# K cache rows of 4 KB in two half loads, and scores on four column groups: an attention decode step on one Trainium2 core

## The chip, the core and the metric

The kernel runs on one core of one Trainium2 chip. The metric is the time of one execution on the device, in microseconds; the smaller the better. Times of a kernel are medians of several executions, and the profile is that of one execution.

## What is computed

One decode step of attention with grouped heads: 32 batches of one query each, 32 query heads of 128 over 8 K/V heads, and a window of the last W = 512 keys of a cache of 2048.

```python
q = (x @ wq).reshape(B, 1, 32, 128).transpose(0, 2, 1, 3)      # x: (32, 1, 512)
k = jnp.repeat(k_cache[:, :, 2048 - 512:, :], 4, axis=1)       # cache: (32, 8, 2048, 128)
v = jnp.repeat(v_cache[:, :, 2048 - 512:, :], 4, axis=1)
scores = jnp.einsum("bhqd,bhkd->bhqk", q, k) * 128 ** -0.5
o = jnp.einsum("bhqk,bhkd->bhqd", softmax(scores), v)
out = o.transpose(0, 2, 1, 3).reshape(B, 1, 4096) @ wo         # wo: (4096, 512)
```

All tensors are bfloat16. Per batch the window is 1 MB of K and 1 MB of V; the weights are 4 MB each. Nothing is used twice, so some 75 MB are read once.

## The kernel before, in words

The order of the work is written out by hand, engine by engine, and held together by semaphores; each engine goes through its own program in order.

**SP** issues all loads on one queue (L118 to L163): x, then K of batch 0, the four pieces of wq, V of batch 0, then for each further batch K and V, then the four pieces of wo. K has NK = 4 slots: `load_k(b)` (L129) waits, before it issues, until the transposes of batch b-4 have read their slot (`pe_T3`). V has NV = 12 slots; `load_v(b)` (L137) waits for the P·V of batch b-12. K is laid out with the key on the partition: partition p holds keys 4p to 4p+3 of each of the 8 heads, so a load of K is 128 x 8 rows of 4 keys x 128 x 2 bytes = 1 KB (L132 to L135). V has the same layout and the same 1 KB rows (L142), wo has rows of 512 x 2 bytes = 1 KB (L149), and wq has rows of 1024 x 2 bytes = 2 KB (L124).

**TensorE** makes q (`qt_pass`, L207), and then works batch by batch. `transposes(b)` (L222) turns the K tile of a batch with 32 transposes of 128 x 128 into four PSUM banks of two heads each (`KT_ps`). `s_matmuls(b)` (L242) computes the scores: for each of the 8 heads one matmul whose stationary operand is `QBD`, 128 x 32, with the four queries of that head in four of the 32 columns and zeros elsewhere, and whose moving operand is the head's transposed K, 128 x 512. All eight add up in the same 32 partitions, 32j to 32j+31 for the j-th batch of a quad (j = b mod 4), which is one of the four column groups of the array. Four batches, a quad, so fill the 128 partitions of one `S_ps` bank. Once per quad, behind the transposes of the next quad's second batch, come the four transposes of the probabilities (`pt_transposes`, L262) and then 128 small matmuls with V (`pv_matmuls`, L274). At the end wo is multiplied in, 32 matmuls of 128 x 512 on four column groups in turn (L315), and a last matmul adds the four partial results (L324).

**VectorE** copies three of the four banks of each batch from PSUM to `KT_sb`, 512 columns at a time (L348); **ScalarE** copies the fourth (L405). `KT_sb` has NKT = 3 slots; the copies of batch b wait for the scores of batch b-3. Once per quad, behind the copies of the next quad's first batch, VectorE finds the row maximum (`softmax_a`, L354), ScalarE takes the exponential (L413), and VectorE scales by the reciprocal of the sum (`softmax_b`, L364); ScalarE copies the transposed probabilities (L422) and VectorE the outputs (L370).

**GpSimd** writes the queries of batch b into the diagonal places of `QBD` (L191), which has 8 slots and was set to zero once (L173).

Of the kernel before, what the change touches and what calls it, by code (L numbers as in the profile page):

```python
# [12 lines left out]
def bass_standalone__sliding_block_cached__sampling_kernel(  # L13
# [11 lines left out]
    HQ = HD // DH  # L25
# [17 lines left out]
    with ExitStack() as es:  # L43
# [4 lines left out]
        K_sb = es.enter_context(nc.sbuf_tensor([P, NK, G, KT * DH], BF16))  # L48
        V_sb = es.enter_context(nc.sbuf_tensor([P, NVA, G, KT * DH], BF16))
        KT_sb = es.enter_context(nc.sbuf_tensor([P, NKT, G, W], BF16))  # L50
# [7 lines left out]
        ident = es.enter_context(nc.sbuf_tensor([P, P], BF16))  # L58
        X_sb = es.enter_context(nc.sbuf_tensor([P, D], BF16))
# [15 lines left out]
        sem_k = [es.enter_context(nc.semaphore(f"sem_k{i}")) for i in range(NK)]  # L75
# [15 lines left out]
        pool_R = es.enter_context(nc.semaphore("pool_R"))  # L91
        dve_xT = es.enter_context(nc.semaphore("dve_xT"))
# [21 lines left out]

        def quad_of(b):
            return b // 4

        @block.sync  # L118
        def _(sp):
# [9 lines left out]
            def load_k(b):  # L129
                if b >= NK:  # L130
                    sp.wait_ge(pe_T3, b - NK + 1)
                sp.dma_start(  # L132
                    K_sb[:, b % NK, :, :],
                    k_cache[b, :, SK - W:, :].rearrange("g (p kt) d -> p g (kt d)", kt=KT),
                ).then_inc(sem_k[b % NK], 16)  # L135
# [30 lines left out]
        def _(pool):  # L166
# [5 lines left out]
            ).then_inc(pool_init, 1)  # L172
            pool.memset(QBD[:, :, :, :], 0.0).then_inc(pool_init, 1)  # L173
# [11 lines left out]
            for b in range(B):  # L185
                if b >= NQB:
                    pool.wait_ge(pe_Sb, b - NQB + 1)
                n = b % NQB
                dst = bass.AP(tensor=QBD, offset=n * G * 32, ap=[[qbd_row, P], [36, G], [1, REP]])
                src = bass.AP(tensor=QT_sb, offset=b * HQ, ap=[[qt_row, P], [REP, G], [1, REP]])  # L190
                pool.tensor_copy(dst, src).then_inc(pool_qbd, 1)  # L191

        @block.tensor
        def _(pe):
# [27 lines left out]
            def transposes(b):  # L222
                pe.wait_ge(sem_k[b % NK], 16 * (b // NK + 1))
                for t in range(4):
                    if b >= 1:
                        if t < 3:
                            pe.wait_ge(dve_T, 6 * (b - 1) + 2 * (t + 1))
                        else:
                            pe.wait_ge(act_T, 2 * b)
                    last = None  # L230
                    for half in range(2):
                        g = 2 * t + half
                        for kt in range(KT):
                            last = pe.matmul(  # L234
                                KT_ps[:, t, half * 512 + kt * 128: half * 512 + (kt + 1) * 128],
                                lhsT=K_sb[:, b % NK, g, kt * DH:(kt + 1) * DH],
                                rhs=ident[:, :],
                                start=True, stop=True, is_transpose=True, tile_position=(0, 0),
                            )
                    last.then_inc(pe_T[t], 1)  # L240

            def s_matmuls(b):  # L242
                q = quad_of(b)
                j = b % 4
                pe.wait_ge(pool_qbd, b + 1)
                if j == 0 and q >= 2:
                    pe.wait_ge(act_exp, q - 1)
                last = None
                for g in range(G):
                    if g < 6:  # L250
                        pe.wait_ge(dve_T, 6 * b + g + 1)
                    else:
                        pe.wait_ge(act_T, 2 * b + (g - 6) + 1)
                    last = pe.matmul(  # L254
                        S_ps[32 * j:32 * (j + 1), q % 2, :],
                        lhsT=QBD[:, b % NQB, g, :],
                        rhs=KT_sb[:, b % NKT, g, :],
                        start=(g == 0), stop=(g == G - 1), tile_position=(0, 32 * j),
                    )
                last.then_inc(pe_Sb, 1)  # L260
# [13 lines left out]
            def pv_matmuls(qq):  # L274
# [6 lines left out]
                for j in range(4):  # L281
                    b = 4 * qq + j
                    pe.wait_ge(sem_v[b % NV], 16 * (b // NV + 1))
                    for g in range(G):
                        for kt in range(KT):
# [3 lines left out]
                                rhs=PT_sb[:, qq % 2, kt * 128 + j * 32 + 4 * g: kt * 128 + j * 32 + 4 * g + 4],  # L289
# [8 lines left out]
            s_matmuls(0)  # L298
            for b in range(1, B):
# [4 lines left out]
                s_matmuls(b)  # L304
                if j == 1 and q >= 1:
                    pv_matmuls(q - 1)
            pt_transposes(NQUAD - 1)
# [21 lines left out]
        def _(dve):  # L329
# [11 lines left out]
            def kt_evacs(b):  # L341
                if b >= NKT:
                    dve.wait_ge(pe_Sb, b - NKT + 1)
                for t in range(3):
                    dve.wait_ge(pe_T[t], b + 1)
                    for half in range(2):
                        g = 2 * t + half
                        dve.tensor_copy(  # L348
                            KT_sb[:, b % NKT, g, :], KT_ps[:, t, half * 512:(half + 1) * 512]
                        ).then_inc(dve_T, 1)  # L350
# [7 lines left out]
            def softmax_b(qq):  # L358
# [3 lines left out]
                if qq >= 2:  # L362
                    dve.wait_ge(pe_PT, qq - 1)
                dve.tensor_scalar(  # L364
                    P_bf[:, qq % 2, :], P_f32[:, qq % 2, :], recip[:, qq:qq + 1], None, op0=ALU.mult
# [28 lines left out]
        def _(act):  # L394
# [3 lines left out]
            def kt_evacs(b):  # L398
                if b >= NKT:
                    act.wait_ge(pe_Sb, b - NKT + 1)  # L400
                for t in range(3, 4):
                    act.wait_ge(pe_T[t], b + 1)
                    for half in range(2):
                        g = 2 * t + half
                        act.activation(  # L405
                            KT_sb[:, b % NKT, g, :], KT_ps[:, t, half * 512:(half + 1) * 512], ACTF.Copy
                        ).then_inc(act_T, 1)
# [62 lines left out]
```

## Time and profile before

| what | us |
|---|---|
| median of 3 runs | 229.69 |
| lowest and highest run | 229.09, 232.55 |
| span of the profiled execution | 228.2 |
| last load (wo, fourth piece) lands at | 222.46 |
| TensorE busy | 176.6 |
| VectorE busy | 90.0 |
| ScalarE busy | 48.1 |

No own time is listed for the profiled execution beside its span; against the median of the runs, what lies around the span comes to 229.69 - 228.2 = 1.5 us, and against the lowest run to 0.9 us.

How to read it: the page gives the busy time of each engine, then the span in 40 slices of 5.7 us with the busy share of each engine in tenths, the granted clock of TensorE, the share of the 16 DMA engines and what they moved in GB/s. The chain that ended last is followed back from the last instruction. A group of instructions is one row: line, engine, operation, what it writes and reads, shape and count; then busy time, mean duration of one in ns, and the idle time before it with what ended it.

### The profile page before, as it was taken

The numbers are of one execution on the slowest core, as the hardware profiler recorded it, in microseconds if no ns is written. First come the engines' busy times: TensorE is split into PE (matmuls) and PEld (weight loads), VectorE is DVE, ScalarE is ACT, GpSimd is POOL, SyncE is SP. The second block draws the span as 40 slices with busy tenths as digits, with TensorE's granted clock in tenths as the row PEclk, the third lists the DMA queues.
The fourth block names the chain that finished last, engine by engine and source line by source line (L and its number), as shares of the span: only waits on it lengthen the run. The fifth ranks groups of instructions, "written<-read, shape, count | busy, mean of one in ns | idle before, by whom it ended". The sixth has DMA issues, their size and how long they took to land.

```text
span 228.2 us, 5628 instructions
## 1 busy us (share of the span) xinstructions
PE 176.6 (77%) x2501; PEld 124.7 (55%) x2501; DVE 90.0 (39%) x237; ACT 48.1 (21%) x93; POOL 9.4 (4%) x43
## 2 busy tenths in 40 slices
PE   0184968669869986995997996699669799999482
PEld 0182555447635753575564964477437656695340
DVE  0047333351535243633275243524353317644212
ACT  2000103122113211320133021321132013403203
POOL 5002000000000000000000000000000000000000
PEclk9998879999997999797699889889997859979855
DMA  6999999999999999999999999999999999999950
GB/s 188 386 385 348 348 348 349 348 348 350 349 347 348 349 347 348 348 348 348 348 348 348 347 348 348 348 348 348 347 347 348 347 348 347 349 345 329 350 183 6
DMA packets 72950, 75.90 MB, mean 333 GB/s; under 512 B 1184, under 2 KB 70880, under 8 KB 72928
## 3 DMA queue, kind: packets, MB, share of 16 engines
q1 hardware_dynamic: 72928, 75.57, 103.7%
q8 instruction: 19, 0.31, 0.6%
q14 instruction: 3, 0.02, 0.0%
HBM read 75.53 MB, written 0.03 MB: 331 GB/s over the span
## 4 chain that ended last, share of the span: by engine, by line
DMA 53%; PE 26%; SPq 16%; issue 2%; DVEq 0%; DVE 0%; ACT 0%
DMA K_sb<-in_k_cache_dram 48%; PE KT_ps L234 12%; PE S_ps L254 7%; PE QO_ps L286 6%; SPq L142 6%; DMA wo_sb<-in_wo_dram 5%; SPq L132 5%; SPq L149 4%; SPq L124 2%; PE PT_ps L266 1%; PE KT_ps L315 0%; DVEq L43 0%; DVE X_sb L389 0%; PE QO_ps L324 0%; ACT out_sb L441 0%
## 5 line engine op out<-in xcount | busy, mean ns | idle before, releaser
L234 PE MATMUL KT_ps<-ident,K_sb 128*128 128x128 bf16 x1024 | 74.3, 240 | 29.7 <-DMA K_sb<-in_k_cache_dram 25.6
L348 DVE COPY KT_sb<-KT_ps 128x512 bf16<-128x512 bf16 x192 | 68.0, 418 | 68.0 <-PE KT_ps L234 67.3
L234 PEld LDWEIGHTS KT_ps<-ident,K_sb 128*128 128x128 bf16 x1024 | 67.8, 108 | 42.1 <-DMA K_sb<-in_k_cache_dram 34.9
L254 PE MATMUL S_ps<-KT_sb,QBD 128*32 128x512 bf16 x256 | 68.2, 414 | 2.8 <-POOL QBD L191 2.8
L405 ACT ACTIVATE KT_sb<-KT_ps 128x512 bf16<-128x512 bf16 x64 | 34.7, 594 | 161.6 <-PE KT_ps L234 161.6
L254 PEld LDWEIGHTS S_ps<-KT_sb,QBD 128*32 128x32 bf16 x256 | 23.7, 102 | 34.8 <-issue 8.2
L286 PEld LDWEIGHTS QO_ps<-PT_sb,V_sb 128*128 128x128 bf16 x768 | 20.0, 97 | 3.2 <-ACT PT_sb L422 2.1
L286 PE MATMUL QO_ps<-PT_sb,V_sb 128*128 128x4 bf16 x768 | 20.7, 165 | 0.8 <-ACT PT_sb L422 0.7
L370 DVE CAST oT_sb<-QO_ps 128x128 bf16<-128x128 f32 x8 | 5.8, 719 | 38.8 <-PE QO_ps L286 38.8
L191 POOL COPY QBD<-QT_sb 128x32 bf16<-128x32 bf16 x32 | 6.3, 209 | 152.7 <-PE S_ps L254 135.8
L214 PE MATMUL QO_ps<-xT_sb,big_sb 128*128 128x32 bf16 x128 | 4.1, 185 | 8.4 <-DMA big_sb<-in_wq_dram 8.3
L336 DVE CAST QT_sb<-QO_ps 128x512 bf16<-128x512 f32 x2 | 4.8, 2393 | 13.0 <-PE QO_ps L214 13.0
L214 PEld LDWEIGHTS QO_ps<-xT_sb,big_sb 128*128 128x128 bf16 x128 | 3.8, 103 | 8.7 <-issue 6.7
L286 PEld LDWEIGHTS QO_ps<-PT_sb,big_sb 128*128 128x128 bf16 x256 | 6.5, 96 | 0.8 <-ACT PT_sb L422 0.8
L286 PE MATMUL QO_ps<-PT_sb,big_sb 128*128 128x4 bf16 x256 | 6.7, 164 | 0.0
L413 ACT ACTIVATE P_f_56<-S_ps,negmax 128x512 f32<-128x512 f32 x8 | 5.5, 687 | 4.0 <-DVE negmax L356 4.0
L354 DVE TENSOR_REDUCE maxv<-S_ps 128x1 f32<-128x512 f32 x8 | 5.5, 682 | 1.0 <-PE S_ps L254 1.0
L266 PE MATMUL PT_ps<-ident,P_bf 128*128 128x128 bf16 x32 | 3.6, 242 | 2.5 <-DVE P_bf L364 2.5
L422 ACT ACTIVATE PT_sb<-PT_ps 128x512 bf16<-128x512 bf16 x8 | 4.8, 604 | 1.2 <-PE PT_ps L266 1.2
L315 PE MATMUL KT_ps<-wo_sb,oT_sb 128*32 128x512 bf16 x32 | 3.9, 626 | 0.9 <-DVE oT_sb L370 0.8
L266 PEld LDWEIGHTS PT_ps<-ident,P_bf 128*128 128x128 bf16 x32 | 2.5, 111 | 3.0 <-DVE P_bf L364 3.0
L364 DVE TENSOR_SCALAR P_bf<-P_f_56,recip 128x512 bf16<-128x512 f32 x8 | 3.9, 486 | 0.3
(25 smaller groups left out, 14.7 us busy)
## 6 DMA issues: line engine op xcount, KB each, us to landing
K_sb<-in_k_cache_dram SPq DMA_DIRECT2D x32, 1024.0 KB, 12.1
V_sb<-in_v_cache_dram SPq DMA_DIRECT2D x24, 1024.0 KB, 12.0
big_sb<-in_v_cache_dram SPq DMA_DIRECT2D x8, 1024.0 KB, 12.0
big_sb<-in_wq_dram SPq DMA_DIRECT2D x4, 1024.0 KB, 10.8
wo_sb<-in_wo_dram SPq DMA_DIRECT2D x4, 1024.0 KB, 12.0
x_sb<-in_x_dram SPq DMA_DIRECT2D x1, 32.0 KB, 1.6
out_dram<-out_sb SPq DMA_DIRECT2D x1, 32.0 KB, 1.5
```

The lines of the kernel that those rows point to most:

```text
L132: sp.dma_start(K_sb[:, b % NK, :, :], k_cache[b, :, SK - W:, :].rearrange("g (p kt) d -> p g (kt d)", kt=KT),).then_inc(sem_k[b % NK], 16)
L142: sp.dma_start(v_slot(b)[:, :, :], v_cache[b, :, SK - W:, :].rearrange("g (p kt) d -> p g (kt d)", kt=KT),).then_inc(sem_v[b % NV], 16)
L149: sp.dma_start(wo_sb[:, c * 8:(c + 1) * 8, :], wo[c * 1024:(c + 1) * 1024, :].rearrange("(h d) n -> d h n", d=P),).then_inc(sem_wo[c], 16)
L191: pool.tensor_copy(dst, src).then_inc(pool_qbd, 1)
L214: last = pe.matmul(QO_ps[:, hl * 32:(hl + 1) * 32], lhsT=wq_sb[:, kt, h * DH:(h + 1) * DH], rhs=xT_sb[:, kt, :], start=(kt == 0), stop=(kt ...
L234: last = pe.matmul(KT_ps[:, t, half * 512 + kt * 128: half * 512 + (kt + 1) * 128], lhsT=K_sb[:, b % NK, g, kt * DH:(kt + 1) * DH], rhs=id ...
L254: last = pe.matmul(S_ps[32 * j:32 * (j + 1), q % 2, :], lhsT=QBD[:, b % NQB, g, :], rhs=KT_sb[:, b % NKT, g, :], start=(g == 0), stop=(g = ...
L266: last = pe.matmul(PT_ps[:, kt * 128:(kt + 1) * 128], lhsT=P_bf[:, qq % 2, kt * 128:(kt + 1) * 128], rhs=ident[:, :], start=True, stop=Tru ...
L286: last = pe.matmul(QO_ps[:, j * 32 + 4 * g: j * 32 + 4 * g + 4], lhsT=v_slot(b)[:, g, kt * DH:(kt + 1) * DH], rhs=PT_sb[:, qq % 2, kt * 12 ...
L348: dve.tensor_copy(KT_sb[:, b % NKT, g, :], KT_ps[:, t, half * 512:(half + 1) * 512]).then_inc(dve_T, 1)
L370: dve.tensor_copy(oT_sb[:, :, 4 * qq:4 * qq + 4].rearrange("p h j -> p j h"), QO_ps[:, 0:128].rearrange("p (j h) -> p j h", h=HQ),).then_i ...
L405: act.activation(KT_sb[:, b % NKT, g, :], KT_ps[:, t, half * 512:(half + 1) * 512], ACTF.Copy).then_inc(act_T, 1)
```

## The change

K of one batch comes in two DMAs of four heads each. Within a half, the partition is no longer a block of keys for all heads, but the pair (block of 16 keys, head): partition 4s + g holds keys 16s to 16s+15 of head g, 16 x 128 x 2 bytes = 4 KB that lie together in the cache. Each half has a semaphore of its own, and the first two banks of transposes wait for the first half only, the last two for the second. A transpose of 128 columns now holds one key of each of the 32 blocks of four heads; it is made against a permutation matrix (`perm`, built by GpSimd at the start) which sorts its output into head, then block. A half therefore lies in `KT_sb` as 16 keys x 4 heads x 32 blocks, and the moving operand of a score matmul is 16 pieces of 32 elements, 128 elements apart. The keys of a score row are then in the order (key in block, block); the scaling of the probabilities, which reads P_f32 and writes P_bf, puts them back into the order of V, by reading with a step.

The scores of head g go to the 32 partitions of column group g mod 4, and within it to rows 16(g div 4) + 4j for the batch j of the quad. The sum over PSUM runs over the four batches of a quad and two heads, and the rows of a quad are sorted differently (`prow`).

VectorE and ScalarE copy a whole bank of 1024 columns at once (three copies and one per batch instead of six and two). And `s_matmuls(b - 1)` stands behind `transposes(b)`; before, `s_matmuls(b)` stood behind `transposes(b)`.

The diff, cut to its core:

```diff
         def load_k(b):
             if b >= NK:
                 sp.wait_ge(pe_T3, b - NK + 1)
-            sp.dma_start(
-                K_sb[:, b % NK, :, :],
-                k_cache[b, :, SK - W:, :].rearrange("g (p kt) d -> p g (kt d)", kt=KT),
-            ).then_inc(sem_k[b % NK], 16)
+            for h in range(2):
+                sp.dma_start(
+                    K_sb[:, b % NK, h * 16 * DH:(h + 1) * 16 * DH],
+                    k_cache[b, 4 * h:4 * h + 4, SK - W:, :].rearrange("g (s r) d -> s g (r d)", s=32),
+                ).then_inc(sem_k[b % NK][h], 16)
...
+            pool.memset(perm[:, :, :], 0.0).then_inc(pool_perm, 1)
+            pool.wait_ge(pool_perm, 1)
+            pool.affine_select(
+                out=perm[:, :, :], in_=perm[:, :, :], compare_op=ALU.not_equal, fill=1.0,
+                base=0, pattern=[[-1, 4], [-4, 32]], channel_multiplier=1,
+            ).then_inc(pool_perm, 1)
...
         def transposes(b):
-            pe.wait_ge(sem_k[b % NK], 16 * (b // NK + 1))
             for t in range(4):
+                if t % 2 == 0:
+                    pe.wait_ge(sem_k[b % NK][t // 2], 16 * (b // NK + 1))
...
-                            rhs=ident[:, :],
+                        rhs=perm[:, :, :],
...
         def s_matmuls(b):
...
+            pe.wait_ge(dve_T, 3 * b + 3)
+            pe.wait_ge(act_T, b + 1)
             for g in range(G):
-                if g < 6:
-                    pe.wait_ge(dve_T, 6 * b + g + 1)
-                else:
-                    pe.wait_ge(act_T, 2 * b + (g - 6) + 1)
                 last = pe.matmul(
-                    S_ps[32 * j:32 * (j + 1), q % 2, :],
+                    S_ps[32 * (g % 4):32 * (g % 4) + 32, q % 2, :],
                     lhsT=QBD[:, b % NQB, g, :],
-                    rhs=KT_sb[:, b % NKT, g, :],
-                    start=(g == 0), stop=(g == G - 1), tile_position=(0, 32 * j),
+                    rhs=KT_sb[:, b % NKT, g // 4, :, g % 4, :],
+                    start=(j == 0 and g < 4), stop=(j == 3 and g >= 4), tile_position=(0, 32 * (g % 4)),
                 )
...
-        s_matmuls(0)
         for b in range(1, B):
             q, j = divmod(b, 4)
             transposes(b)
             if j == 1 and q >= 1:
                 pt_transposes(q - 1)
-            s_matmuls(b)
+            s_matmuls(b - 1)
             if j == 1 and q >= 1:
                 pv_matmuls(q - 1)
+        s_matmuls(B - 1)
         pt_transposes(NQUAD - 1)
         pv_matmuls(NQUAD - 1)
...
             for t in range(3):
                 dve.wait_ge(pe_T[t], b + 1)
-                for half in range(2):
-                    g = 2 * t + half
-                    dve.tensor_copy(
-                        KT_sb[:, b % NKT, g, :], KT_ps[:, t, half * 512:(half + 1) * 512]
-                    ).then_inc(dve_T, 1)
+                dve.tensor_copy(
+                    KT_sb[:, b % NKT, t // 2, 8 * (t % 2):8 * (t % 2) + 8, :, :], KT_ps[:, t, :]
+                ).then_inc(dve_T, 1)
...
             dve.tensor_scalar(
-                P_bf[:, qq % 2, :], P_f32[:, qq % 2, :], recip[:, qq:qq + 1], None, op0=ALU.mult
+                P_bf[:, qq % 2, :].rearrange("p (kt s u) -> p kt s u", kt=KT, s=32),
+                P_f32[:, qq % 2, :].rearrange("p (u kt s) -> p kt s u", kt=KT, s=32),
+                recip[:, qq:qq + 1], None, op0=ALU.mult,
             ).then_inc(dve_P, 1)
```

How the change moves instructions, at three places. First the start of SP's queue; a row is a line, the destination and source, and the shape in partitions x rows x elements. Before:

```order
L120 DMA x_sb<-in_x_dram 32x512
L132 DMA K_sb<-in_k_cache_dram 128x8x512
L124 DMA big_sb<-in_wq_dram 128x4x1024 x4
L142 DMA V_sb<-in_v_cache_dram 128x8x512
L132 DMA K_sb<-in_k_cache_dram 128x8x512
```

and now:

```order
L125 DMA x_sb<-in_x_dram 32x512
L138 DMA K_sb<-in_k_cache_dram 128x1x2048 x2
L129 DMA big_sb<-in_wq_dram 128x4x1024 x4
L148 DMA V_sb<-in_v_cache_dram 128x8x512
L138 DMA K_sb<-in_k_cache_dram 128x1x2048 x2
```

The order of the loads is the same; a K load of 8 rows of 512 elements per partition has become two of one row of 2048.

Second the start of TensorE's program: x transposed, the two passes of q (`QO_ps`), the transposes of K (`KT_ps`) and the scores (`S_ps`). Before:

```order
L198 MATMUL S_ps<-ident,x_sb 128x32 x4
L214 MATMUL QO_ps<-xT_sb,big_sb 128x32 x64
L234 MATMUL KT_ps<-ident,K_sb 128x128 x32
L214 MATMUL QO_ps<-xT_sb,big_sb 128x32 x64
L254 MATMUL S_ps<-KT_sb,QBD 32x512 x8
L234 MATMUL KT_ps<-ident,K_sb 128x128 x32
```

and now:

```order
L215 MATMUL S_ps<-ident,x_sb 128x32 x4
L231 MATMUL QO_ps<-xT_sb,big_sb 128x32 x64
L253 MATMUL KT_ps<-perm,K_sb 128x128 x32
L231 MATMUL QO_ps<-xT_sb,big_sb 128x32 x64
L253 MATMUL KT_ps<-perm,K_sb 128x128 x32
L271 MATMUL S_ps<-KT_sb,QBD 32x512 x8
```

The scores of batch 0 have moved behind the transposes of batch 1, and so all through: each batch's scores stand behind the next batch's transposes.

Third the end of TensorE's program, from the transposes of batch 31 on. Before:

```order
L234 MATMUL KT_ps<-ident,K_sb 128x128 x32
L254 MATMUL S_ps<-KT_sb,QBD 32x512 x8
L266 MATMUL PT_ps<-ident,P_bf 128x128 x4
L286 MATMUL QO_ps<-PT_sb,V_sb 128x4 x128
L315 MATMUL KT_ps<-wo_sb,oT_sb 32x512 x32
L324 MATMUL QO_ps<-X_sb,R_sb 32x512
```

and now:

```order
L253 MATMUL KT_ps<-perm,K_sb 128x128 x32
L271 MATMUL S_ps<-KT_sb,QBD 32x512 x16
L283 MATMUL PT_ps<-ident,P_bf 128x128 x4
L303 MATMUL QO_ps<-PT_sb,V_sb 128x4 x128
L332 MATMUL KT_ps<-wo_sb,oT_sb 32x512 x32
L341 MATMUL QO_ps<-X_sb,R_sb 32x512
```

Between the last transposes and the softmax of the last quad there are now the scores of two batches, 30 and 31, instead of one.

50 lines of the change are left out of this document (29 added, 21 removed).

## The prediction

> **What bounds the kernel now.** First I read the page: the busy time of the engines, the two lines on the DMA engines, and the chain that ended last.
>
> ```profile
> span 228.2 us, 5628 instructions
> ...
> PE 176.6 (77%) x2501; PEld 124.7 (55%) x2501; DVE 90.0 (39%) x237; ACT 48.1 (21%) x93; POOL 9.4 (4%) x43
> ...
> DMA  6999999999999999999999999999999999999950
> GB/s 188 386 385 348 348 348 349 348 348 350 349 347 348 349 347 348 348 348 348 348 348 348 347 348 348 348 348 348 347 347 348 347 348 347 349 345 329 350 183 6
> ...
> DMA 53%; PE 26%; SPq 16%; issue 2%; DVEq 0%; DVE 0%; ACT 0%
> ```
>
> From the second slice to the 38th the DMA engines are never under 90% busy, and for some 190 us they move the same 348 GB/s. Nothing else in the page is so even. TensorE stands in the chain with 26%, so the next question is whether it ever holds the loads up. The steady stretch of SP's queue, in order of time (start, duration, instruction):
>
> ```profile
> 161.68 2.92 SPq L142 DMA_DIRECT2D V_sb<-in_v_cache_dram  x1
> 164.64 2.90 SPq L132 DMA_DIRECT2D K_sb<-in_k_cache_dram  x1
> 167.59 2.90 SPq L142 DMA_DIRECT2D V_sb<-in_v_cache_dram  x1
> ```
>
> SP issues load after load without a gap, 2.9 us each, the time that 1.049 MB take at 348 GB/s (3.01 us). At the start, with empty queues, the same instruction took less:
>
> ```profile
> 1.19 0.41 SPq L132 DMA_DIRECT2D K_sb<-in_k_cache_dram  x1
> ```
>
> and the page's list of DMA issues (count, size, us to landing):
>
> ```profile
> K_sb<-in_k_cache_dram SPq DMA_DIRECT2D x32, 1024.0 KB, 12.1
> ```
>
> 0.41 us against 2.9: the issue isn't slow, it waits for room. 12.1 us from issue to landing are four loads in flight. So the stream of loads is full, SP is ahead of it, and the kernel ends when 75.5 MB have passed. **What sets the rate** is seen in the mean over two stretches: 30 to 200 us, where K and V pass in 1 KB rows, and 6 to 16 us, where wq passes in 2 KB rows.
>
> ```profile
> DMA packets 58399, 59.15 MB, mean 348 GB/s; under 512 B 902, under 2 KB 58380, under 8 KB 58380
> ...
> DMA packets 1938, 3.87 MB, mean 387 GB/s; under 512 B 50, under 2 KB 50, under 8 KB 1938
> ```
>
> Both times the engines are full, and the rate differs with the packet. One engine of 16 spends 1024 x 16 / 348 = 47.1 ns on a packet of 1 KB and 2048 x 16 / 387 = 84.7 ns on one of 2 KB: 37.6 ns for each KB and about 9.5 ns for the packet itself.
>
> **The loads of K.** 32 x 1.049 = 33.55 MB are 32768 packets of 1 KB, 2048 on each engine: 2048 x 47.1 = 96.5 us of the stream. Now they are 8192 packets of 4 KB, 512 on each. The trace has no such packet. Bounds: if 2 KB already reaches a ceiling, K passes at 387 GB/s, 86.7 us; if the 9.5 ns vanish too, 4 x 37.6 = 150.4 ns, 77.0 us. I take the straight line through the two rows, 84.7 + 2 x 37.6 = 159.9 ns (410 GB/s): 512 x 159.9 = 81.9 us, a gain of **14.6 us** (9.8 to 19.5). [...]
>
> 32 more DMAs bring 32 more of the small packets per engine that follow a load. Each costs nothing to 47.1 ns; with four bytes it is nearest to the 9.5 ns of a packet without its KBs: **+0.3 us** (0 to 1.5). SP issues twice as many loads of K, at 0.41 us where there is room: 32 more are 13 us of a queue that has some 210; they are hidden while SP is ahead.
>
> **The scores on four column groups.** Before and after are compared in these groups (busy us, mean ns; idle before):
>
> ```profile
> L234 PE MATMUL KT_ps<-ident,K_sb 128*128 128x128 bf16 x1024 | 74.3, 240 | 29.7 <-DMA K_sb<-in_k_cache_dram 25.6 <-issue 4.0
> L254 PE MATMUL S_ps<-KT_sb,QBD 128*32 128x512 bf16 x256 | 68.2, 414 | 2.8 <-POOL QBD L191 2.8
> L348 DVE COPY KT_sb<-KT_ps 128x512 bf16<-128x512 bf16 x192 | 68.0, 418 | 68.0 <-PE KT_ps L234 67.3
> L405 ACT ACTIVATE KT_sb<-KT_ps 128x512 bf16<-128x512 bf16 x64 | 34.7, 594 | 161.6 <-PE KT_ps L234 161.6
> L364 DVE TENSOR_SCALAR P_bf<-P_f_56,recip 128x512 bf16<-128x512 f32 x8 | 3.9, 486 | 0.3
> L336 DVE CAST QT_sb<-QO_ps 128x512 bf16<-128x512 f32 x2 | 4.8, 2393 | 13.0 <-PE QO_ps L214 13.0
> ```
>
> The transposes already idle 25.6 us for K. What four groups bring is seen at the end, where the matmuls with wo go round the four groups, at a granted clock of 0.50 (the number before the last two in the stage's row):
>
> ```profile
> 220.02 0.16 PEld L315 LDWEIGHTS KT_ps<-wo_sb,oT_sb 128*32 128x32 bf16 x4 [0.27 <-issue]
> 220.44 0.16 PEld L315 LDWEIGHTS KT_ps<-wo_sb,oT_sb 128*32 128x32 bf16 x4 [0.27 <-issue]
> ```
>
> ```profile
> 220.00:228.20 8.20, 4.08 (x33) 0.97 (x25) 1.36 (x2) 1.76 (x3) 0.00 (x0) 0.50 0.06 18
> ```
>
> Four matmuls every 0.43 us at half clock, so the eight of a batch take 0.85 us, and half of that at full clock, where L254 takes 68.2 / 32 = 2.1 us now. TensorE loses 41 to 54 us of work. It stands beside the loads: a batch needs 2.6 + 3.0 = 5.6 us of the stream (before 6.0). The parts of a quad, as long as they were at half clock, where the transposes took 3.43 us instead of 1.96:
>
> ```profile
> 170.51 3.43 PE L234 MATMUL KT_ps<-ident,K_sb 128*128 128x128 bf16 x32 [2.18 <-DMA K_sb<-in_k_cache_dram]
> ...
> 173.73 0.59 PE L266 MATMUL PT_ps<-ident,P_bf 128*128 128x128 bf16 x4
> ...
> 176.09 3.36 PE L286 MATMUL QO_ps<-PT_sb,big_sb 128*128 128x4 bf16 x128
> ```
>
> A whole quad at half clock: 4 x (3.43 + 0.85) + 0.59 + 3.36 = 21.1 us, against 4 x 5.6 = 22.4 us of loads. So the scores are worth **0 us**, since the loads cover them. If the cover were gone they would count in full. The moving operand in pieces of 32 elements has no row; below it is no slower, above as slow as the stepped copy L336, 4.67 ns an element. Pieces of 64 bytes are nearer to contiguous; I take no loss.
>
> **Waits and moves.** `s_matmuls(b-1)` now stands behind the wait for K of batch b, and so starts up to 5.6 us later. Who waits: the softmax, but on VectorE it stands behind the copies of that same batch b anyway; the copies, which need the scores of three batches back; and `QBD` with 8 slots. 0 us each. `load_k(b)` waits for the transposes of b-4, with up to three pairs of loads (16.7 us) behind that batch; V has 12 slots. Loads of K now hold fewer packets, so SP will run further ahead and really stand in this wait, at no cost. The copies of 1024 columns cost at most two of 512; VectorE is busy 90 of 228 us. `perm` is built while TensorE waits for wq. 0 us.
>
> **The end.** From the last K on, TensorE's rows, and the chain's row of the last wo:
>
> ```profile
> 207.86 1.96 PE L234 MATMUL KT_ps<-ident,K_sb 128*128 128x128 bf16 x32 [0.53 <-DMA K_sb<-in_k_cache_dram]
> 209.75 1.90 PE L254 MATMUL S_ps<-KT_sb,QBD 128*32 128x512 bf16 x8
> 214.15 0.40 PE L266 MATMUL PT_ps<-ident,P_bf 128*128 128x128 bf16 x4 [2.50 <-DVE P_bf L364]
> ...
> 219.61 3.93 PE L315 MATMUL KT_ps<-wo_sb,oT_sb 128*32 128x512 bf16 x32 [0.80 <-DVE oT_sb L370]
> ```
>
> ```profile
> 210.95 11.51 DMA wo_sb<-in_wo_dram
> ```
>
> wo's last piece lands at 222.46, 14.6 us behind the last K, and so it will stay, since V and wo are unchanged. The computation has a chain beside that: 11.75 us from 207.86 to 219.61, then six rounds of four matmuls at 0.43 us, 14.3 us in all. It has only 0.3 us to spare. Changes in it: half of the transposes wait for the last half load (-0.98 us), the scores of two batches stand between instead of one (2 x 0.43 to 2 x 0.85 plus the wait for a 1.08 us copy, against 1.9: 0 to +0.9), and the stepped read of the probabilities (L364) costs 0.49 us as now up to 2.39 as L336, 0 to +1.9. Together -1.0 to +1.8; I take 0, since L364 keeps its contiguous write, which L336 lacks.
>
> **Sum.** Span 228.2 - 14.6 + 0.3 = 213.9 us. Around the span lie 1.5 us to the median of the runs: **215.4 us**, 6% less.
>
> **Rivals.** *The rate has a ceiling at 387 GB/s.* For it: only that rate is seen, and it may be the memory's and not the packet's. Against: it is a step of the size that a fixed cost per packet gives. Gain 9.8, with the small packets 229.7 - 9.8 + 0.3 = **220.2 us**.
>
> *Packets of 4 KB bring nothing*, because they are cut into 1 KB after all, or K's place in memory limits it to what it has: K stays at 348 GB/s, **230.0 us**. Against: wq's rows arrive as packets of their full 2 KB, and order and DMA shape say one row of 2048 elements. [...]
>
> *The big packets are slower*, since four heads that lie 512 KB apart (2048 x 128 x 2 bytes) are read by turns and get in each other's way. Its place is K's share of the stream; it decides from 188 ns a packet (4 x 47.1), where K gains nothing. The only bigger packets in the trace are the 16 KB of instruction loads:
>
> ```profile
> q8 instruction: 19, 0.31, 0.6%
> ```
>
> 0.6% of 16 x 228.2 us over 19 packets is 1.15 us each, 0.29 us for 4 KB; at that price K takes 147 us, the kernel **281 us**. Against: K and V before have the same step between heads, and run as fast as wo, which has not (351 GB/s):
>
> ```profile
> 210.00:215.00 5.00, 2.04 (x12) 0.78 (x10) 2.16 (x7) 2.19 (x5) 0.00 (x0) 1.00 1.08 351
> ```
>
> [...]
>
> **Chances.** The forecast 0.79; the ceiling 0.11; nothing gained 0.06; slower 0.04. The first two are both faster by over 2% (under 225.1 us; 2% is about what a measurement of this kernel can tell from no change): 0.90 faster, 0.06 the same, 0.04 slower. The range takes in the ceiling and half of the way to the upper gain: **213 to 220.5 us**; the forecast's own is 213 to 217.5.
>
> **What would show it.** Right: some 49 thousand packets instead of 72.9 thousand, those under 2 KB down from 70.9 to some 38.6 thousand; 2.097 MB in 5.6 us, some 376 GB/s, in the middle slices; the last wo landing near 208 us; score matmuls busy under 30 us; waits of SP for the transposes with gaps between its issues, and DMA slices still full. Wrong: slices at 348 or about 366 GB/s (ceiling); slices under 9 in the middle, which would mean that TensorE holds the loads up; and for the end, wo landed long before its last matmuls start.

## The result, and the profile after

The changed kernel takes **217.37 us** (median of 4 runs, 217.21 to 217.76) against 229.47 us before (median of 4, 229.09 to 232.55): a ratio of 0.948, 95% interval 0.9466 to 0.9495. The forecast was 215.4 us, the range 213 to 220.5. Ratios here and below leave out executions more than 1.5% above the fastest of their kernel, so they are not quite the quotient of the medians.

The page of the kernel after: busy time, the 40 slices, the packets, and the chain that ended last.

```profile
span 215.7 us, 5573 instructions
...
PE 149.2 (69%) x2501; PEld 120.0 (56%) x2501; DVE 89.7 (42%) x141; ACT 46.3 (21%) x61; POOL 10.0 (5%) x45
...
DMA  5999999999999999999999999999999999999910
GB/s 166 369 397 374 375 376 375 375 375 375 375 378 376 377 376 378 378 377 376 377 377 375 378 376 378 373 377 377 375 377 377 376 372 376 376 366 319 354 67 6
DMA packets 48886, 75.91 MB, mean 352 GB/s; under 512 B 1696, under 2 KB 38624, under 8 KB 48864
...
DMA 41%; PE 34%; SPq 13%; issue 5%; ACT 4%; DVE 1%; DVEq 0%; ACTq 0%
```

The DMA line is as full as it was, slice by slice, and every slice in the middle now moves 372 to 378 GB/s instead of some 348. The packets are 24 thousand fewer, and those under 2 KB have gone from 70880 to 38624: K's 32768 are gone, 8192 larger ones and 512 small ones have come. The mean over the even stretch (30 to 185 us):

```profile
DMA packets 36720, 58.32 MB, mean 376 GB/s; under 512 B 1328, under 2 KB 29602, under 8 KB 36701
```

A pair of K and V, 2.097 MB, takes 2.097 / 376 = 5.58 us; 3.01 of them are V's, taken at the 348 GB/s of before, so 2.57 us are left for the 16 packets of 4 KB of each engine: 160 ns a packet. The groups that answer to those of before:

```profile
L253 PE MATMUL KT_ps<-perm,K_sb 128*128 128x128 bf16 x1024 | 90.7, 266 | 39.5 <-DMA K_sb<-in_k_cache_dram 32.9
L363 DVE COPY KT_sb<-KT_ps 128x1024 bf16<-128x1024 bf16 x96 | 63.8, 690 | 50.2 <-PE KT_ps L253 49.0
L420 ACT ACTIVATE KT_sb<-KT_ps 128x1024 bf16<-128x1024 bf16 x32 | 32.8, 1024 | 148.7 <-PE KT_ps L253 148.7
L271 PE MATMUL S_ps<-KT_sb,QBD 128*32 128x512 bf16 x256 | 23.3, 446 | 0.7 <-ACT KT_sb L420 0.7
L379 DVE TENSOR_SCALAR P_bf<-P_f,recip 128x512 bf16<-128x512 f32 x8 | 5.9, 742 | 0.3
```

The scores take 23.3 us instead of 68.2, but TensorE as a whole only 27 us less: its transposes went from 74.3 to 90.7 us. They are as many and of the same shape; the granted clock of TensorE is lower (0.785 on average against 0.882), with 149.2 us busy instead of 176.6. TensorE still waits for K, 32.9 us. SP's queue in the steady state:

```profile
162.39 0.59 SPq L148 DMA_DIRECT2D V_sb<-in_v_cache_dram  x1
163.02 5.08 SPq L138 DMA_DIRECT2D K_sb<-in_k_cache_dram  x2
168.15 0.59 SPq L148 DMA_DIRECT2D V_sb<-in_v_cache_dram  x1
```

V's issue takes 0.59 us instead of 2.9, but the two issues of K take 5.1, and again there is no gap between one row and the next: SP's time has moved from V to K. Part of K's time is `load_k`'s wait for the transposes, which the forecast named. The view of SP's waits (us in total, times, longest) has it before, and now:

```profile
SPq L132 <- PE KT_ps L234: 39.8, 19, 3.5
```

```profile
SPq L138 <- PE KT_ps L253: 51.4, 16, 4.4
```

So SP stood in this wait before the change too; the forecast took its 2.9 us for a wait for room alone. The wait is 12 us longer now, and the DMA slices stay full behind it.

At the end: the last wo, and TensorE's rows from the last transposes on (the first two rows are from the view of one line: issues of wo from first to last, and time to landing, of which the last one's is the least).

```profile
L155 SPq DMA_DIRECT2D wo_sb<-in_wo_dram x4: 2802/3702/5020, 185.1 to 197.6; - x4
...
DMA to landing us min/median/max: 11.3/12.8/15.2
```

```profile
193.44 2.61 PE L253 MATMUL KT_ps<-perm,K_sb 128*128 128x128 bf16 x32
195.97 0.62 PE L271 MATMUL S_ps<-KT_sb,QBD 128*32 128x512 bf16 x8
197.31 0.61 PE L271 MATMUL S_ps<-KT_sb,QBD 128*32 128x512 bf16 x8 [0.72 <-ACT KT_sb L420]
200.69 0.40 PE L283 MATMUL PT_ps<-ident,P_bf 128*128 128x128 bf16 x4 [2.77 <-DVE P_bf L379]
...
206.16 0.62 PE L332 MATMUL KT_ps<-wo_sb,oT_sb 128*32 128x512 bf16 x3 [0.80 <-DVE oT_sb L387]
207.43 3.59 PE L332 MATMUL KT_ps<-wo_sb,oT_sb 128*32 128x512 bf16 x29 [0.66 <-issue]
```

The last wo lands at 197.6 + 11.3 = 208.9 us, and the last matmul with wo ends at 207.43 + 3.59 = 211.0, 2.1 us later; before it was 223.6 - 222.5 = 1.1 us. In this execution TensorE no longer waits for wo at the end: wo waits for TensorE.

### The profile page after: what moved, and what is told of

Read it like the earlier page. It is cut to its first block, busy times and chain, and to the rows that moved or that the text cites. A ratio compares the mean times of both kernels' runs of the same rounds, so it can differ in the third digit from the quotient of the medians.

```text
span 215.7 us, 5573 instructions
## 1 busy us (share of the span) xinstructions
PE 149.2 (69%) x2501; PEld 120.0 (56%) x2501; DVE 89.7 (42%) x141; ACT 46.3 (21%) x61; POOL 10.0 (5%) x45
## 2 busy tenths in 40 slices
DMA packets 48886, 75.91 MB, mean 352 GB/s; under 512 B 1696, under 2 KB 38624, under 8 KB 48864
## 4 chain that ended last, share of the span: by engine, by line
DMA 41%; PE 34%; SPq 13%; issue 5%; ACT 4%; DVE 1%; DVEq 0%; ACTq 0%
DMA K_sb<-in_k_cache_dram 41%; PE KT_ps L253 18%; PE QO_ps L303 13%; SPq L138 10%; SPq L148 3%; ACT PT_sb L437 2%; PE KT_ps L332 2%; ACT KT_sb L420 2%; SPq L129 1%; PE S_ps L271 1%; DVE P_bf L379 0%; DVEq L43 0%; DVE oT_sb L387 0%; DVE maxv L369 0%; DVE X_sb L406 0%
## 5 line engine op out<-in xcount | busy, mean ns | idle before, releaser
L253 PE MATMUL KT_ps<-perm,K_sb 128*128 128x128 bf16 x1024 | 90.7, 266 | 39.5 <-DMA K_sb<-in_k_cache_dram 32.9
L253 PEld LDWEIGHTS KT_ps<-perm,K_sb 128*128 128x128 bf16 x1024 | 81.8, 123 | 56.1 <-DMA K_sb<-in_k_cache_dram 48.1
L363 DVE COPY KT_sb<-KT_ps 128x1024 bf16<-128x1024 bf16 x96 | 63.8, 690 | 50.2 <-PE KT_ps L253 49.0
L420 ACT ACTIVATE KT_sb<-KT_ps 128x1024 bf16<-128x1024 bf16 x32 | 32.8, 1024 | 148.7 <-PE KT_ps L253 148.7
L271 PE MATMUL S_ps<-KT_sb,QBD 128*32 128x512 bf16 x256 | 23.3, 446 | 0.7 <-ACT KT_sb L420 0.7
L271 PEld LDWEIGHTS S_ps<-KT_sb,QBD 128*32 128x32 bf16 x256 | 4.0, 98 | 5.4 <-issue 3.3
L428 ACT ACTIVATE P_f<-S_ps,negmax 128x512 f32<-128x512 f32 x8 | 5.5, 687 | 4.5 <-DVE negmax L371 4.5
L379 DVE TENSOR_SCALAR P_bf<-P_f,recip 128x512 bf16<-128x512 f32 x8 | 5.9, 742 | 0.3
```

The source lines that it names most:

```text
L253: last = pe.matmul(KT_ps[:, t, i * 128:(i + 1) * 128], lhsT=K_sb[:, b % NK, r * DH:(r + 1) * DH], rhs=perm[:, :, :], start=True, stop=True ...
L271: last = pe.matmul(S_ps[32 * (g % 4):32 * (g % 4) + 32, q % 2, :], lhsT=QBD[:, b % NQB, g, :], rhs=KT_sb[:, b % NKT, g // 4, :, g % 4, :], ...
L363: dve.tensor_copy(KT_sb[:, b % NKT, t // 2, 8 * (t % 2):8 * (t % 2) + 8, :, :], KT_ps[:, t, :]).then_inc(dve_T, 1)
L420: act.activation(KT_sb[:, b % NKT, t // 2, 8 * (t % 2):8 * (t % 2) + 8, :, :], KT_ps[:, t, :], ACTF.Copy).then_inc(act_T, 1)
```

## The experiments

Two theories could explain the 12 us. **Packets:** the loads set the pace, and an engine spends 9.5 ns on a packet and 37.6 ns on each KB of it. **TensorE:** the time came from the scores on four groups. A third was open for the size: a **ceiling** of the rate near what was seen.

### The groups alone, with the old loads

The change with K's load, its place in memory and the transposes against the identity as before:

```diff
-                for h in range(2):
-                    sp.dma_start(
-                        K_sb[:, b % NK, h * 16 * DH:(h + 1) * 16 * DH],
-                        k_cache[b, 4 * h:4 * h + 4, SK - W:, :].rearrange("g (s r) d -> s g (r d)", s=32),
-                    ).then_inc(sem_k[b % NK][h], 16)
+                sp.dma_start(
+                    K_sb[:, b % NK, :, :],
+                    k_cache[b, :, SK - W:, :].rearrange("g (p kt) d -> p g (kt d)", kt=KT),
+                ).then_inc(sem_k[b % NK][0], 16)
...
-                            rhs=perm[:, :, :],
+                            rhs=ident[:, :],
...
-                        rhs=KT_sb[:, b % NKT, g // 4, :, g % 4, :],
+                        rhs=KT_sb[:, b % NKT, g, :],
```

> The other part of the change alone: scores on four column groups, one batch late, and copies of 1024 columns as in the change, but K in one load of 1 KB rows with the key on the partition, as before. Theory (packets: an engine spends 9.5 ns on a packet and 37.6 ns on each KB): K's packets are back at 47.1 ns for 1 KB, which gives back 14.6 - 0.3 us, so 229 to 232 us, with 348 GB/s in the middle, although TensorE keeps its short scores (about 23 us busy instead of 68). Rival (TensorE: the time came from the scores): stays at 217 to 219 us.

Measured: 229.62 us (10 runs), ratio to before 0.9996, interval 0.9978 to 1.0014. The scores' group, and the mean of 30 to 185 us:

```profile
L268 PE MATMUL S_ps<-KT_sb,QBD 128*32 128x512 bf16 x256 | 24.0, 460 | 0.7 <-ACT KT_sb L415 0.7
```

```profile
DMA packets 53373, 54.04 MB, mean 349 GB/s; under 512 B 823, under 2 KB 53357, under 8 KB 53357
```

TensorE has lost 44 us of scores (its transposes, at 92.2 us, took 18 of them back) and the kernel's time is the same within 0.2%. The TensorE theory falls.

### The loads alone, with one column group

The change with `QBD`, the output rows and the sums of the scores as before, one group of 32 partitions for each batch:

```diff
-                        S_ps[32 * (g % 4):32 * (g % 4) + 32, q % 2, :],
+                        S_ps[32 * j:32 * (j + 1), q % 2, :],
...
-                        start=(j == 0 and g < 4), stop=(j == 3 and g >= 4), tile_position=(0, 32 * (g % 4)),
+                        start=(g == 0), stop=(g == G - 1), tile_position=(0, 32 * j),
...
-            return 32 * (g % 4) + 16 * (g // 4) + 4 * j
+            return 32 * j + 4 * g
```

> The change's loads of K alone: 4 KB rows in two halves, but all eight score matmuls of a batch in one column group, 32j, as before. Theory (packets): the loads still set the pace, 376 GB/s in the middle; a quad of TensorE is 4 x (1.96 + 2.1) + 4 = 20 us at full clock against 22.4 us of loads, hidden; at the end two batches of scores stand in the chain, each 1.3 us longer, of which about 0.5 us hides behind a copy: 218 to 220.5 us. Rival (TensorE): 228 to 231 us, like the kernel before.

Measured: 219.53 us, ratio 0.9562, interval 0.9531 to 0.9593.

```profile
L266 PE MATMUL S_ps<-KT_sb,QBD 128*32 128x512 bf16 x256 | 63.2, 394 | 0.0
```

```profile
DMA packets 36747, 58.36 MB, mean 377 GB/s; under 512 B 1330, under 2 KB 29624, under 8 KB 36728
```

With 63 us of scores the loads run at the same 377 GB/s. So 10.2 of the 12.1 us come without the groups; the groups bring the other 2 us, and only together with the loads. In the two profiles 1.6 us of that show at the end: in this kernel two batches of scores stand behind the last transposes with 1.6 us each, and the first matmul with wo starts at 207.8 us instead of 206.2:

```profile
196.32 3.22 PE L266 MATMUL S_ps<-KT_sb,QBD 128*32 128x512 bf16 x16
...
207.77 0.61 PE L327 MATMUL KT_ps<-wo_sb,oT_sb 128*32 128x512 bf16 x3 [0.81 <-DVE oT_sb L382]
```

### Rows of 2 KB

Each half in two loads of 2 KB rows, four DMAs for a K:

```diff
-                    sp.dma_start(
-                        K_sb[:, b % NK, h * 16 * DH:(h + 1) * 16 * DH],
-                        k_cache[b, 4 * h:4 * h + 4, SK - W:, :].rearrange("g (s r) d -> s g (r d)", s=32),
-                    ).then_inc(sem_k[b % NK][h], 16)
+                    for c in range(2):
+                        sp.dma_start(
+                            K_sb[:, b % NK, (2 * h + c) * 8 * DH:(2 * h + c + 1) * 8 * DH],
+                            k_cache[b, 4 * h:4 * h + 4, SK - W:, :].rearrange(
+                                "g (s c r) d -> c s g (r d)", s=32, c=2
+                            )[c],
+                        ).then_inc(sem_k[b % NK][h], 16)
...
```

> The change with each half load of K cut into two loads of 2 KB rows; K lies in the same places. Theory (9.5 ns a packet, 37.6 ns a KB): 1024 packets of 84.7 ns on each engine instead of 512 of 159.9, 4.8 us more, and 64 more small packets per engine at about 10 ns, 0.6 us more: 222 to 223.5 us, some 364 GB/s in the middle. Rival (a ceiling that 2 KB packets already reach): 217.4 to 218.5 us. Rival (TensorE): 217.4 us.

Measured: 222.99 us, ratio 0.9713, interval 0.9667 to 0.9759.

```profile
DMA packets 43563, 56.77 MB, mean 366 GB/s; under 512 B 2151, under 2 KB 29773, under 8 KB 43545
```

2.097 / 366 - 3.01 = 2.72 us for 32 packets, 85 ns each: the row of wq in the profile before (84.7 ns). No ceiling at 2 KB; the forecast's first rival falls.

### Rows of 8 KB

One load for a K, 16 blocks of 32 keys x 8 heads on the partitions:

```diff
-                for h in range(2):
-                    sp.dma_start(
-                        K_sb[:, b % NK, h * 16 * DH:(h + 1) * 16 * DH],
-                        k_cache[b, 4 * h:4 * h + 4, SK - W:, :].rearrange("g (s r) d -> s g (r d)", s=32),
-                    ).then_inc(sem_k[b % NK][h], 16)
+                sp.dma_start(
+                    K_sb[:, b % NK, :],
+                    k_cache[b, :, SK - W:, :].rearrange("g (s r) d -> s g (r d)", s=16),
+                ).then_inc(sem_k[b % NK][0], 16)
...
```

> The line drawn one step further: K in one load of 8 KB rows, 16 blocks of 32 keys x 8 heads on the partitions, everything else as in the change. Theory (9.5 ns a packet, 37.6 ns a KB): 256 packets of 310 ns on each engine, 79.4 us instead of 81.9, and 32 small packets fewer: 2.8 us less for the loads, less 0 to 1 us at the end, where the transposes wait for a whole load: 214.5 to 216 us, some 382 GB/s in the middle. Rival (a ceiling near 410 GB/s): 217 to 218.5 us.

Measured: **330.62 us** (325.92 to 337.32), ratio 1.4255. Both expectations were wrong. The mean of 60 to 260 us:

```profile
DMA packets 26522, 46.91 MB, mean 235 GB/s; under 512 B 714, under 2 KB 23678, under 8 KB 23678
```

The engines are full, over 90% busy in 39 of the stretch's 40 slices, and slow: in the packet records one of 8 KB lasts 581 ns on average, and even V's packets of 1 KB beside them 71 ns instead of 50. Something in the order of the reads, or in the size of the rows, gets in its own way. Four more kernels look for it, all from this one.

The same places, each row cut into two loads of 4 KB:

```diff
-                sp.dma_start(
-                    K_sb[:, b % NK, :],
-                    k_cache[b, :, SK - W:, :].rearrange("g (s r) d -> s g (r d)", s=16),
-                ).then_inc(sem_k[b % NK][0], 16)
+                for c in range(2):
+                    sp.dma_start(
+                        K_sb[:, b % NK, c * 16 * DH:(c + 1) * 16 * DH],
+                        k_cache[b, :, SK - W:, :].rearrange("g (s c r) d -> c s g (r d)", s=16, c=2)[c],
+                    ).then_inc(sem_k[b % NK][0], 16)
...
```

> The kernel with 8 KB rows, each row cut into two loads of 4 KB rows; every partition keeps its place in the cache, 16 blocks of 32 keys x 8 heads. Theory 1 (it was the packet of 8 KB that was slow, 581 ns on average): packets of 4 KB at 160 ns are back and so is the change's time, 217 to 219 us. Theory 2 (it was the order in which the engines go through the cache, eight heads 512 KB apart by turns): the packets stay slow, 290 ns or so for 4 KB, and the time stays near 330 us, in any case above 260.

Measured: 311.41 us (308.52 to 328.81). Packets of 4 KB are slow here, 279 ns on average in the records of the slowest of the four executions (328.81 us), against 168 in those of the change. So packets of 4 KB alone are no cure.

Eight KB, but four heads by turns:

```diff
-                sp.dma_start(
-                    K_sb[:, b % NK, :],
-                    k_cache[b, :, SK - W:, :].rearrange("g (s r) d -> s g (r d)", s=16),
-                ).then_inc(sem_k[b % NK][0], 16)
+                for h in range(2):
+                    sp.dma_start(
+                        K_sb[64 * h:64 * h + 64, b % NK, :],
+                        k_cache[b, 4 * h:4 * h + 4, SK - W:, :].rearrange("g (s r) d -> s g (r d)", s=16),
+                    ).then_inc(sem_k[b % NK][0], 16)
...
```

> Rows of 8 KB again, but in two loads of four heads each (64 partitions, 16 blocks of 32 keys x 4 heads), so that an engine goes through four heads 512 KB apart by turns and not eight; the rest is as in the kernel with 8 KB rows. Theory 1 (eight heads by turns are what is slow, and four are not): packets of 310 ns, the line of 9.5 ns and 37.6 ns a KB holds up to 8 KB: 214 to 217 us. Theory 2 (steps of 8 KB from engine to engine, or rows of 8 KB, are what is slow, whatever the number of heads): 300 us or more. Between the two, 225 to 290 us: the number of heads counts, but so does the rest.

Measured: 302.95 us (291.14 to 306.15). Four heads by turns alone are no cure either. The turns are those of the rows in the load; which rows an engine takes shows in no view. The change, which is fast, has both, packets of 4 KB and four heads, and its blocks lie 4 KB apart and not 8; which of these it takes together, no run separates.

Pieces 128 KB apart instead of heads 512 KB apart (near), and, from that, rows in one run with no such steps (flat). Neither loads the right keys; the two read the same 1 MB for a batch, in the same rows of 8 KB, and differ in nothing but the order of the rows:

```diff
+                near = k_cache[b, 0:2, :, :].rearrange("a t d -> (a t d)")
                 sp.dma_start(
-                    K_sb[:, b % NK, :],
-                    k_cache[b, :, SK - W:, :].rearrange("g (s r) d -> s g (r d)", s=16),
+                    K_sb[:, b % NK, :], near.rearrange("(g s f) -> s g f", g=8, s=16),
                 ).then_inc(sem_k[b % NK][0], 16)
```

```diff
-                    K_sb[:, b % NK, :], near.rearrange("(g s f) -> s g f", g=8, s=16),
+                    K_sb[:, b % NK, :], near.rearrange("(p f) -> p f", p=P),
```

> The kernel with one load of K in 8 KB rows, but what it loads as the eight heads of a batch are eight neighbouring pieces of 128 KB of the cache instead of eight pieces 512 KB apart. It leaves the right keys out, so only its time is read. Theory 1 (the step of 512 KB between rows that follow each other is what is slow once rows are long): packets of 310 ns, 214 to 217 us. Theory 2 (rows of 8 KB are slow whatever they lie beside): 300 us or more.

> The same once more, with the rows of 8 KB taken straight through 1 MB of the cache, each partition behind the one before. It leaves the right keys out, so only its time is read. Theory 1 (the step of 512 KB is slow): 214 to 217 us, as with the step of 128 KB. Theory 2 (rows of 8 KB are slow): 300 us or more. If this one is fast and the one with a step of 128 KB isn't, the large step between rows counts, whatever its size.

Measured: near 332.8 us (328.23 and 337.37), flat **214.39 us** (214.34 and 214.44; ratio 0.9348, interval 0.9313 to 0.9382). Near first, then flat, 60 to 260 and 30 to 185 us:

```profile
DMA packets 25703, 45.43 MB, mean 227 GB/s; under 512 B 695, under 2 KB 22952, under 8 KB 22952
```

```profile
DMA packets 33064, 59.11 MB, mean 381 GB/s; under 512 B 900, under 2 KB 29431, under 8 KB 29431
```

Read straight through, 8 KB rows are on the line: 2.097 / 381 - 3.01 = 2.49 us for 8 packets, 311 ns each, where the line says 310. Read in turns over heads 512 KB apart they cost nearly twice that (581 ns in the packet records, where the flat ones show 325), and with pieces 128 KB apart the mean rate is as low (227 GB/s against 235). The same bytes in packets of the same size take 333 us in one order and 214 in the other. So long rows are not slow in themselves, and large steps alone are not (by their layout V steps 512 KB from each row of 1 KB to the next, and the change itself from each row of 4 KB); 16 blocks of 8 KB by turns with large steps are. Why that order is slow, and which reads meet in it, the traces don't show: that stays open. The repeated runs of these slow kernels scatter by 3 to 7%, so nothing is read from the differences among them.

### K one place earlier in the queue

```diff
+            load_k(1)
             load_v(0)
             for b in range(1, B):
-                load_k(b)
+                if b + 1 < B:
+                    load_k(b + 1)
                 load_v(b)
```

> The change, with each load of K put one place earlier in SP's queue, ahead of the V of the batch before, so that the last K lands some 2.6 to 3 us earlier against the last wo. Theory (the end is set by the later of two: the landing of wo, and TensorE's chain behind the last K, which came out some 1 us too late in the change's profile): the chain gets out of the way and the last matmul with wo ends 1.1 us behind wo's landing instead of 2.15: 216.2 to 217.4 us. Rival (the chain costs nothing, the 2 us that the forecast lacked lie in the loads): 217.1 to 217.7 us, with the last wo landing as late as before and its matmuls as late behind it.

Measured: **215.87 us** (215.71 to 215.94), ratio 0.939, interval 0.937 to 0.9409, 0.3 us below the theory's lower end. The chain of waits now ends as it did before the change, with wo:

```profile
196.89 11.26 DMA wo_sb<-in_wo_dram
208.15 0.04 issue
208.19 1.08 PE KT_ps L334 x8
```

Its last wo lands at 208.15 and the last matmul with it ends 1.1 us later. The span is 213.9 to 214.2 us against 214.8 to 215.7 of the change. So in the change's profile the computation behind the last K was the later of the two at the end, and cost about 1 us of span. The two profiled spans differ by 1.8 us; the rest is wo's landing, at 208.15 us instead of 208.89. In the other executions the spans differ by some 0.8 us, and how that divides isn't known. The time fell by some 0.7 us more than the span; what lies around the span shows in no view.

### The scores directly behind their transposes

```diff
+            s_matmuls(0)
             for b in range(1, B):
...
-                s_matmuls(b - 1)
+                s_matmuls(b)
...
-            s_matmuls(B - 1)
```

> The change, with the scores of a batch directly behind its own transposes again. Theory (the loads cover TensorE): TensorE waits about 1.1 us in each batch for the copy of the last bank, hidden behind the loads; at the end one batch of scores less stands in the chain, 0.6 us, but the wait for the copy is the same: 216.8 to 217.8 us. Rival (the late scores are what keeps TensorE ahead of the loads): slower, from 32 x 0.3 us on, 220 us or more.

Measured: 218.05 us, 0.25 us above the theory's upper end, the runs in two groups, 216.65 to 217.04 and 219.07 to 219.33, for which the profile, that of a run of the first group, shows no cause; ratio 0.9483, interval 0.9444 to 0.9523, which holds the change's 0.948. A cost of 3 us and more is excluded; whether the late scores do a little good or harm stays open.

### V in longer rows too

The line carried on to the other half of the traffic: K one place earlier, and V in 2 KB rows, 64 blocks of 8 keys x 2 heads on the partitions.

```diff
+                for t in range(4):
+                    g0 = 4 * (t // 2) + t % 2
+                    sp.dma_start(
+                        v_slot(b)[:, t * 8 * DH:(t + 1) * 8 * DH],
+                        v_cache[b, g0:g0 + 3:2, SK - W:, :].rearrange("e (s r) d -> s e (r d)", s=64),
+                    ).then_inc(sem_v[b % NV], 16)
...
+                            last = pe.matmul(
+                                bass.AP(tensor=QO_ps, offset=j * 32 + 4 * g0, ap=[[512, P], [8, 2], [1, 4]]),
+                                lhsT=v_slot(b)[:, (8 * t + r) * DH:(8 * t + r + 1) * DH],
...
+                for e in range(2):
+                    w = slice(64 * e, 64 * e + 64)
+                    last = dve.tensor_scalar(
+                        P_bf[w, qq % 2, :, :, e].rearrange("p r (s u) -> p r s u", u=2),
+                        P_f32[w, qq % 2, :].rearrange("p (u r s) -> p r s u", u=2, s=32),
+                        recip[w, qq:qq + 1], None, op0=ALU.mult,
+                    )
```

> Not an experiment on the change's parts but the packet theory carried on to V: the change with K one place earlier in the queue, and V in 2 KB rows, 64 blocks of 8 keys x 2 heads on the partitions, in four loads per batch. The probabilities get a column for each block and head, zero where the head is not that of the row, so that one matmul takes two heads; 8 transposes of probabilities per quad instead of 4, two scalings on VectorE instead of one, V slots 11 instead of 12. Theory (9.5 ns a packet, 37.6 ns a KB): V's packets cost 1024 x 84.7 = 86.7 us on each engine instead of 2048 x 47.1 = 96.5, 9.7 us less, and 96 more small packets at 10 ns, 1 us more: 207.5 to 210 us, some 394 GB/s in the middle. Rival (at a pair of loads in 5.3 us TensorE, at half clock much of the time, becomes the bound): 212 us or more, DMA slices under 9.

Measured: **206.85 us** (206.64 to 207.75), ratio 0.9006, interval 0.8983 to 0.9029: faster than both kernels, and 0.65 us below the theory's lower end. The mean of 30 to 185 us:

```profile
DMA packets 25765, 61.46 MB, mean 396 GB/s; under 512 B 2813, under 2 KB 3305, under 8 KB 25746
```

A pair now takes 2.097 / 396 = 5.30 us, as the two packet prices say (16 x 160 + 32 x 85 ns = 5.28).

## Why the prediction was right, point by point

**The bound.** Right. The groups alone, with 44 us less of scores, changed the time by less than its error; the change without the groups brought 10.2 us, and cutting K's rows from 4 KB to 2, with nothing else changed, gave 5.6 us back.

**The price of a packet of 4 KB.** Right: 160 ns against 159.9, drawn as a line through two rows of the profile before. It holds at 2 KB (85 ns), at 8 KB read straight through (311 ns), and for V (a pair in 5.30 us where the prices say 5.28).

**The scores, the waits, the copies at nothing.** Right in sum. The forecast had covered TensorE at half clock; the half clock came more often (a granted clock under 0.6 in 9 of the 40 slices, before in 3), the transposes rose by 16 us, and it cost nothing in the middle, where the DMA slices stay over 90% at 372 to 378 GB/s. SP's wait for the transposes, 51.4 us now and 39.8 before, starves no slice. That SP would begin to stand in it only now was wrong, and the gaps between its issues that were to show it don't appear.

**What the sum missed:** 2.0 us for the median, 2.4 for the profiled execution, which took 217.76. In the profiled execution these are three small terms, all of one sign.

The last wo landed at 208.9 instead of 222.5 - 14.3 = 208.2: 0.7 us. In the kernels with K earlier and with the scores directly behind their transposes it landed at 208.15 and 208.17, so this is within the scatter of single executions.

The end was put at no change, in a range of -1.0 to +1.8; it came to +1.0. There is a pause of TensorE in front of the fourth matmul with wo, for which the profile names no cause. It shows as 0.66 us, but it costs more: the 32 matmuls take 4.86 us with it, from 206.16 to 211.02, at a granted clock of 0.50, and 3.60 without it in the kernel with flat rows of 8 KB, 0.45 us for four, about the pace at half clock before (0.43):

```profile
204.31 3.60 PE L331 MATMUL KT_ps<-wo_sb,oT_sb 128*32 128x512 bf16 x32 [0.80 <-DVE oT_sb L386]
```

By that, an estimate, they would have been done at 209.8 without the pause, 0.9 us behind wo's landing, and the landing would have decided as before. So the pause is enough for the whole +1.0; the stepped read of the probabilities (742 ns instead of 486, near the low end of its bounds) would by the same estimate not have shown alone.

And what lies around the span was taken from the median of before less the span of one execution, 1.5 us. The later runs list both for each execution: 2.1 us before, 2.1 to 2.6 after. Executions of before with a span of 228.2, that of the profile, take 230.3 us, some 0.6 more than the median: the sum set the span of a slower execution beside the time of a median one, and the term was mis-sized by 0.6 us.

For the median the 2.0 us divide otherwise: the three other executions of the change have spans of 214.8 to 214.9, 0.9 to 1.0 above the forecast's 213.9, and 2.4 to 2.6 us around them instead of 1.5.

**The rivals.** The ceiling at 387 GB/s: excluded by rows of 2 KB in their own kernel, 5.6 us slower than rows of 4 KB. Nothing gained: excluded. The slow packets: not at 4 KB in 32 blocks, and so not in this change. But the effect is there one step on: with 16 blocks of 8 KB, 279 ns for a packet of 4 KB (in the execution of 328.81 us), near the 0.29 us that the forecast had taken as its price, and a median of 311 us against the 281 that it had worked out; V's packets suffered too, 75 ns instead of 50. That the price came so near is luck: it was that of instruction loads of 16 KB, which no run connects with this. The argument that spoke against it, that K's and V's 1 KB rows make the same steps and run at 348 GB/s, was too weak: the flat kernel shows that the same rows at other steps are fast, and the change that the same steps with other rows are.

## What to carry to other kernels

Where the DMA slices are full and the rate differs between two stretches with different rows, the price of a packet can be read off as a line (here 47.1 ns at 1 KB and 84.7 at 2 KB), and a change of the row length can be costed from it, here to within 2 us, as long as the order of the reads isn't one of the slow ones; work taken from an engine that the loads cover was worth nothing until the end of the kernel (44 us less of scores with the old loads: ratio 0.9996). A load that jumps between far places must be timed at the very row length and block step it will use: here 4 KB rows in blocks of 4 KB gave 5% and 8 KB rows in blocks of 8 KB lost 43%. When a gain brings two ends together, as wo's landing and the computation behind the last K here, the order of the last loads is worth another look; it gave another 1.5 us.

## What the runs showed of the hardware that was not expected

Long rows, read by turns from places 128 or 512 KB apart in blocks of 8 KB, nearly halve the rate of K: 581 ns for a packet of 8 KB in the packet records, against 325 in those of the flat kernel; the number of places (four or eight) and the size of the packets (4 or 8 KB) change little, each by itself (302.95 us with four, 311.41 with packets of 4 KB, 330.62 with neither). The kernel with 8 KB rows at a step of 512 KB moved 235 GB/s with V's rows among them, but the same step with rows of 4 KB in the change moved 376, and a step of 128 KB was as slow (227) as one of 512.

TensorE's transposes became slower when its scores became shorter: 74.3 us before (granted clock 0.882), 90.7 after (0.785), 75.0 in the kernel that kept its long scores (0.898) and 92.2 in the one that had short scores with the old loads (0.772), in the same number and shape each time. So in these four profiles it goes with the scores and not with the loads.
